# Written order through the last attention chunk, a later routing step and three plane buffers, in an attention + mixture-of-experts kernel

## The chip, the cores and the metric

One core of a Trainium2 chip runs the whole kernel. The metric is device time in microseconds (us) of one execution; lower is better.

## The reference

Eight batches of 1856 rows go through an attention without softmax, the result gates `u`, and all 14848 rows go through a two-level top-1 mixture of 16 experts.

```python
scores = (1 / S) * z @ z.T                      # S = 1856, z: [S, 64]
x = u * (np.maximum(scores, 0) ** 2 @ v)        # u, v: [S, 256]
g_idx = argmax(x @ w_group); e_idx = argmax(x @ w_expert[g_idx])
out = g_w * e_w * (relu(x @ w1[g, e]) @ w2[g, e])   # w1: [256, 1024], w2: [1024, 256]
```

`g_w` and `e_w` are the softmax weights of the chosen group and expert.

## The kernel before

**Attention.** Each batch is cut into four chunks of queries (512, 512, 512 and 320 wide in batches 1 to 7), and each chunk runs over 15 tiles of 128 keys. One key step is one number `s`; there are NS = 480 steps, and the last batch has steps 420 to 479, 15 for each chunk. `attn_v(s)` is TensorE's part (L408): six products, or four where the key tile is the short last one, of 512 or 320 columns. Its operands are the high part `ah` and the low part `al` of the squared scores. They are made six steps ahead by `scores`: for some key tiles from new scores (L370 to L385), for the others from a mirrored tile that an earlier chunk wrote to DRAM and that four DMAs bring back as `at` (`load_mirror`, L326; then `ah` on ScalarE at L359 and `al` on VectorE at L360). In the last chunk (steps 465 to 479, NK = 15) twelve of the fifteen steps use mirrored tiles, and steps 476 to 479 use those of the third mirrored group.

**End of a chunk.** `chunk_end` multiplies by `u` into `xT` (L430, one buffer) and puts off the rest by some steps: `split_x` makes `xh` on ScalarE (L436), `rest_x` makes `xl` on VectorE (L441), `planes` copies `xT` into a plane buffer `pl` on ScalarE (L465) and has SP transpose it into `rows` (L471), `logits` runs four products on TensorE (L483, L484), and `logits_out` copies them out and has SP transpose them into `lgx` (L494). A plane buffer (tag `pl`) also takes the rows of a block of tokens when `load_x` reads them back from the DRAM array `bucket` (L767).

**Routing.** `route` is a generator; `run_gens` lets it advance by a few operations in each step. About 13 small VectorE operations, a pause of 9, 5 or 1 steps, two small products `pk` on TensorE (L610, L611), some more VectorE operations that end in the row numbers `di`, and then one indirect DMA on GpSimd for each 128 rows (L646). The last batch has three such generators, one after the other: chunks 0 and 1 together, chunk 2, chunk 3. After them comes the final sort of the experts.

**Experts.** The first two blocks of tokens (512 rows of each of the two fullest experts) are fixed before the last batch is routed, so they are computed while that routing goes on: `load_rows(0)` and `join_x(0)` (L781 to L787) stand in the last attention steps, `phase1` (L802 to L813) and `phase2_t` (L887) of blocks 0 and 1 follow the attention, with a call of `early` after each eighth of a phase 1 and before each half of a phase 2; a call of `early` is one more step for the generators, four operations at most. What is left of the generators is written out after phase 1 of block 1. The rows of block 2 can be read only when every row of the last batch is in `bucket`.

**What sets the order.** From step 15 on, TensorE, ScalarE and VectorE take their instructions in the order in which the program writes them (`manual_schedule`), up to step 465. Everything after that, and SP and GpSimd throughout, is put in order by a planner: on each engine it takes the instruction that stands first in the program among those that it holds to be ready by its own reckoning of time. From the block pairs (`duo`) on, all engines are in written order again.

Of the kernel before, what the change touches and what calls it, by code (L numbers as in the profile page):

```python
# [9 lines left out]
F32 = mybir.dt.float32  # L10
# [3 lines left out]
U16 = mybir.dt.uint16  # L14
# [5 lines left out]
P = 128  # L20
# [4 lines left out]
def f32(ap):  # L25
    return ap.bitcast(F32)
# [3 lines left out]
def tile_glu_attn_moe(  # L30
# [12 lines left out]
    B, D, S = uT.shape  # L43
    DQ = zT.shape[1] // 2
    NE, _, F = w1.shape
# [5 lines left out]
    NK = NKF + 1  # L51
# [39 lines left out]
    def sb(tag, shape, dt, bufs, name):  # L91
        return pool.tile(shape, dt, tag=tag, bufs=bufs, name=name)
# [19 lines left out]
    def new_rows(name):  # L112
        return sb("rows", [P, 4, RW], I32, 4, name)

    def new_pl(name):
        return sb("pl", [P, 2048], U16, 2, name)

    def new_xhl(name):
        return tuple(new_vb(f"{h}_{name}").rearrange("p (d q) -> p d q", d=ND) for h in ("xh", "xl"))
# [222 lines left out]
    NS = len(steps)  # L342
# [77 lines left out]
    def chunk_end(s):  # L420
        b, c, k = steps[s]
        w = QW[b][c]
        last = s == NS - 1
        nt = (w + P - 1) // P
        oa = oacc.pop(s - k)
        u_t = ut.pop((b, c))
        xT = sb("xT", [P, ND, 512], F32, 1, f"xT_{b}_{c}")[:, :, 0:w]
        xhl = []
        for d in range(ND):
            nc.vector.tensor_mul(out=xT[:, d, :], in0=oa[d][:, 0:w], in1=u_t[:, d, :])  # L430

        def split_x():
            xhl.extend(new_xhl(f"{b}_{c}"))
            xh, xl = xhl
            for d in range(ND):
                nc.scalar.copy(out=xh[:, d, 0:w], in_=xT[:, d, :])  # L436

        def rest_x():
            xh, xl = xhl
            for d in range(ND):  # L440
                nc.vector.tensor_sub(out=xl[:, d, 0:w], in0=xT[:, d, :], in1=f32(xh[:, d, 0:w]))  # L441

        rows = new_rows(f"rows_{b}_{c}")
        nc.gpsimd.iota(rows[:, 0:nt, D + 1:RW], pattern=[[P, nt], [0, RW - D - 1]],
                       base=b * S + QO[b][c], channel_multiplier=1)
        part = w % P
        pl = new_pl(f"pl_{b}_{c}").rearrange("p (t g q) -> p t g q", t=4, q=P)
        lgp = sb("lgp", [P, 512], F32, 1, f"lgp_{b}_{c}").bitcast(U16)[0:LP].rearrange("p (t h q) -> p t h q", t=4, q=P)
        if c % 2 == 0:
            duo[b, c // 2] = (rt_("lgx", [8, 2, LP], f"{b}_{c}", U16), [])  # L450
        lgx2, parts2 = duo[b, c // 2]
        lgx = lgx2[:, 4 * (c % 2):4 * (c % 2) + nt]
        parts2.append((rows, nt, part))
        if nt < 4:
            nc.gpsimd.memset(lgx2[:, 4 * (c % 2) + nt:4 * (c % 2) + 4], 0)
        if part:
            nc.gpsimd.memset(pl[:, nt - 1, :, part:P], 0)
            nc.gpsimd.memset(lgp[:, nt - 1, :, part:P], 0)

        def planes(d):  # L460

            for t0, t1, q in ((0, w // P, P), (w // P, nt, part)):
                if t1 > t0:
                    src = xT[:, d, t0 * P:t0 * P + (t1 - t0) * q].bitcast(U16)
                    nc.scalar.copy(  # L465
                        out=pl[:, t0:t1, 2 * d:2 * d + 2, 0:q],
                        in_=src.rearrange("p (t q h) -> p t h q", q=q, h=2),
                    )
            if d == ND - 1:
                for t in range(nt):  # L470
                    nc.sync.dma_start_transpose(  # L471
                        rows[:, t, 0:D].bitcast(U16).rearrange("p (g d) -> p g d", d=P),
                        pl[:, t].rearrange("p g q -> p (g q)"),
                    )

        pls = []

        def logits():
            ps = bank(ps_m, "m", f"pl_{b}_{c}")
            pls.append(ps)  # L480
            xh, xl = xhl
            for d in range(ND):
                nc.tensor.matmul(ps[0:LP, 0:w], whl[:, d, :], xh[:, d, 0:w], start=(d == 0), stop=False)  # L483
                nc.tensor.matmul(ps[0:LP, 0:w], wh0[:, d, :], xl[:, d, 0:w], start=False, stop=(d == ND - 1))  # L484

        def logits_out():
            ps = pls[0]
            for t0, t1, q in ((0, w // P, P), (w // P, nt, part)):
                if t1 > t0:
                    src = ps[0:LP, t0 * P:t0 * P + (t1 - t0) * q].bitcast(U16)  # L490
                    nc.scalar.copy(
                        out=lgp[:, t0:t1, :, 0:q], in_=src.rearrange("p (t q h) -> p t h q", q=q, h=2)
                    )
            nc.sync.dma_start_transpose(  # L494
                lgx.rearrange("p t h l -> p (t h) l"), lgp[:, 0:nt].rearrange("p t h q -> p (t h q)")
            )

        LG = (7 if b == B - 1 and c < 2 else (9 if c == 2 else 8 if c == 0 else 7)) if s + 1 < NS - NK else 2
        XO = 2 if s + 1 < NS - NK else 0
        (split_x() if XO == 0 else defer(s + XO, split_x))  # L500
        (rest_x() if XO == 0 else defer(s + XO + 1, rest_x))
        PL = XO + 1 if not XO or c == 2 else LG + 2
        defer(s + PL, lambda: planes(0))
        defer(s + PL + 1, lambda: planes(1))
        defer(s + LG, logits)
        defer(s + LG + (1 if XO else 0), logits_out)
        wait = 5 if last else 12 if b == 0 and c < 2 else (17 if c == 1 and b < B - 1 else 15) if s + 1 < NS - NK else 8
        alone = b == B - 1 and c >= NQ - 2
        if c % 2 or alone:
            gens.append((max(s + wait, PFILL[-1] + 2), route(b, c // 2, (c % 2,) if alone else (0, 1))))  # L510
        if last_sort(b, c):
            gens.append((0, sort_experts()))
        if last:
            gens.append((0, sort_experts(final=True)))
# [305 lines left out]
    def phase2(name, wt, hs, meta, n, outs, between=None):  # L820
        nt = (n + P - 1) // P
        held = same if name == "ov" else pin
        for at, t in enumerate([nt - 1] + list(range(nt - 1)) if half(n) else range(nt)):
# [7 lines left out]
            one = name == f"w{NE - 1}_1" and t == nt - 1  # L831
# [7 lines left out]
            for f in range(0 if pair else NF):  # L839
                w2t = wt["2"][f // 2][:, (f % 2) * 512:(f % 2 + 1) * 512]  # L840
                held(nc.tensor.matmul(py[0:m, 0:D], hs[f][1][:, ts], w2t[:, 0:D], start=False, stop=(f == NF - 1)))
            y = sb("yl", [P, D], F32, 3, f"y_{name}_{t}")
            cw = meta[0:m, t, 0:1].bitcast(F32)
            top = py[0:m, 0:D]
            if pair:
# [139 lines left out]
    for b in range(1, B):  # L985
        for what, n, load, cut in PREP if b > 1 else PREP0:
            s0 = (b - 1) * NQ * NK
            begin.setdefault(s0 + load[0] * NK + load[1], []).append((what, b, n))
            split_at.setdefault(s0 + cut[0] * NK + cut[1], []).append((what, b, n))
    WPREP = ((2, (2, 3), (2, 9)), (0, (2, 4), (2, 12)), (1, (2, 5), (2, 14)), (3, (3, 0), (3, 6)))  # L990
    xs = []
    ahead = 4
    for s in range(ahead):
# [7 lines left out]
    for s in range(NS):  # L1001
        b, c, k = steps[s]
        if s == NK:
            region.enter_context(tc.manual_schedule(engines={mybir.EngineType.PE, mybir.EngineType.Activation, mybir.EngineType.DVE}))
        if s == NS - NK:
            region.close()
        if s in (1, 4):
            pz.pop(0)()
        if s in (2, 6, 9):
            pv.pop(0)()  # L1010
        if s == 8:
            make_router()
        for i in range(2 * NE):
            if PFILL[i] == s:
                prefill(i)
        nxt = s // NK + 1
        if k == 3 and nxt < B * NQ:
            load_ut(nxt // NQ, nxt % NQ)
        if b + 1 == B:
            for pc, load, cut in WPREP:  # L1020
                if (c, k) == load:
                    wts.setdefault(0, new_w())
                    prep[pc] = load_w(regs(0)[0], wts[0], pc, "e0")
                if (c, k) == cut:
                    prep.pop(pc)()
        for what, pb, n in begin.get(s, ()):
            prep[(what, n)] = (prep_v if what == "v" else prep_z)(pb, n)
        for what, pb, n in split_at.get(s, ()):
            prep.pop((what, n))()
        if k == (5 if s < NK else 5) and nxt < B * NQ:  # L1030
            prep_zm(nxt // NQ, nxt % NQ)
        if s == NS - NK - 6:
            load_rows(0)
        if s == NS - 6:
            load_rows(1)
        if s == NS - 12:
            xs.append(join_x(0, rows_b[0][0], blocks[0][2]))
        while ahead < min(NS, s + LEAD + 1, max(4, 3 + s + s // 2)):
            scores(ahead)
            ahead += 1  # L1040
        attn_v(s)
        if k == NK - 1:
            chunk_end(s)
        run_deferred(s)
        run_gens(s, 2 if b + 1 < B else (3 if c < 3 else 5))
# [339 lines left out]
    for i, (e, r0, n) in enumerate(blocks):  # L1385
# [20 lines left out]
        last = i + 1 == NB  # L1406
# [67 lines left out]
    for e in range(NOLD, NE):  # L1474
# [36 lines left out]
        B = ("0 0 x0 T2 T4; 0 5 x3 x2l; 0 9 x5 x1; 0 14 x4; 0 18 x6; 1 3 sv; 1 8 sa; 1 11 go; 1 12 m; 1 14 m; 1 18 m; 1 21 m")  # L1511
# [92 lines left out]
```

## Time and profile before

| what | value |
|---|---|
| median of 3 runs | 1426.38 us (1425.99 to 1427.35) |
| the profiled execution, its own time | 1423.95 us |
| its span, first to last instruction | 1422.1 us |
| TensorE (PE) busy | 1411.9 us, 99% of the span |
| VectorE (DVE) busy | 1216.5 us, 86% |
| ScalarE (ACT) busy | 1051.3 us, 74% |
| GpSimd (POOL) busy | 439.0 us, 31% |
| TensorE's granted clock, mean | 1.000 of full speed |

Matmuls are pipelined: each is shown for some 0.3 to 0.4 us, but the next starts after 0.15 to 0.23 us. So a short wait can hide inside a "busy" PE, and the starts of two matmuls say more than the busy time.

### The profile page before, as it was taken

Reading aid. Unit: us, or ns where it says so; the run is one execution under the profiler, and the core shown is the slowest. Engines: PE = TensorE matmul, PEld = TensorE weight load, DVE = VectorE, ACT = ScalarE, POOL = GpSimd, SP = SyncE. Lnnn points to the kernel's source line nnn. Section 1 sums busy time; section 2 is a strip of 40 time slices with the busy share of each in tenths; the row PEclk is TensorE's granted clock in tenths of the full one; section 3 lists DMA queues with packets and bytes.
Section 4 is the critical chain, followed back from the end, with each engine's and each line's share of the span. In section 5 each row is a group of like instructions: output and inputs, shape, how many; then the busy total and the mean of one; then the engine's idle time right before and its main releaser. Section 6 shows DMA issues by size and latency. Waiting matters only on the chain.

```text
span 1422.1 us, 22589 instructions
## 1 busy us (share of the span) xinstructions
PE 1411.9 (99%) x7010; PEld 1223.8 (86%) x7010; DVE 1216.5 (86%) x2436; ACT 1051.3 (74%) x1849; POOL 439.0 (31%) x462
## 2 busy tenths in 40 slices
PE   9999999999999999999999999999999999999998
PEld 7898888888888888888878898988888888899997
DVE  7889999899998999998988667789777888888884
ACT  8887887787887878878776354357777777777773
POOL 0002022220222012202222331332445555555554
PEclk9999999999999999999999999999999999999999
DMA  9997979979899698895987564534555444555552
GB/s 318 328 260 210 235 187 254 230 192 239 195 262 238 160 264 207 223 244 151 243 197 165 116 142 113 122 82 130 126 136 132 126 123 113 138 137 136 139 140 60
DMA packets 400043, 256.47 MB, mean 180 GB/s; under 512 B 244131, under 2 KB 355262, under 8 KB 399920
## 3 DMA queue, kind: packets, MB, share of 16 engines
q1 hardware_dynamic: 387984, 223.97, 63.1%
q0 software_dynamic: 11856, 30.90, 7.7%
q8 instruction: 56, 0.92, 0.3%
q14 instruction: 67, 0.55, 0.1%
q10 hardware_dynamic: 80, 0.13, 0.0%
HBM read 108.29 MB, written 89.21 MB: 139 GB/s over the span
## 4 chain that ended last, share of the span: by engine, by line
PE 92%; DVE 2%; DMA 2%; issue 2%; POOL 1%; ACT 1%; SPq 0%; POOLq 0%; DVEq 0%; ACTq 0%
PE o L408 38%; PE duo_p L887 15%; PE yT L887 6%; PE duo_y L1333 6%; PE sc L370 5%; PE sc L371 5%; PE ph L802 2%; PE ph L803 2%; PE ph L804 2%; PE duo_w L1333 2%; PE duo_x L1333 2%; PE duo_p L1333 2%; PE duo_z L1333 2%; PE pl L483 1%; PE pl L484 1%
## 5 line engine op out<-in xcount | busy, mean ns | idle before, releaser
L408 PE MATMUL o<-ah,vl 128*128 128x512 f32 (+2 forms) x960 | 354.6, 370 | 0.4 <-DVE ah L382 0.4
L408 PE MATMUL o<-ah,vh 128*128 128x512 f32 (+2 forms) x960 | 354.2, 369 | 0.0
L408 PE MATMUL o<-al,vh 128*128 128x512 f32 (+2 forms) x896 | 328.7, 369 | 0.9 <-DVE al L360 0.9
L646 POOL DMA_INDIRECT bucket<-rows,di x121 | 138.6, 1145 | 383.3 <-issue 216.7
L374 ACT ACTIVATE r<-sc 128x512 f32<-128x512 f32 (+2 forms) x312 | 178.8, 573 | 74.4 <-PE sc L371 72.8
L408 PEld LDWEIGHTS o<-ah,vl 128*128 128x128 f32 x960 | 180.2, 188 | 31.0 <-DVE ah L382 1.2
L408 PEld LDWEIGHTS o<-ah,vh 128*128 128x128 f32 x960 | 180.2, 188 | 28.9
L385 DVE TENSOR_TENSOR al<-r,ah 128x512 fp32r<-128x512 f32 (+2 forms) x280 | 187.7, 671 | 19.1 <-ACT r L379 2.2
L930 POOL DMA_INDIRECT out_dram<-y_w,meta_w x92 | 139.3, 1514 | 191.4 <-ACT y_w L924 145.8
L408 PEld LDWEIGHTS o<-al,vh 128*128 128x128 f32 x896 | 167.8, 188 | 27.5 <-DVE al L360 1.2
L887 PE MATMUL duo_p<-hh_w,duo_w 128*128 128x496 f32 (+10 forms) x692 | 178.0, 371 | 0.0
L381 ACT ACTIVATE r<-r 128x512 f32<-128x512 f32 (+2 forms) x280 | 171.4, 612 | 8.9
L887 PEld LDWEIGHTS duo_p<-hh_w,duo_w 128*128 128x128 f32 x692 | 128.6, 188 | 16.7
L382 DVE CAST ah<-r 128x512 fp32r<-128x512 f32 (+2 forms) x280 | 115.9, 414 | 18.8 <-ACT r L381 13.4
L370 PE MATMUL sc<-zm,z2h 128*128 128x512 f32 (+2 forms) x312 | 120.0, 385 | 0.2 <-DVE zm L251 0.2
L371 PE MATMUL sc<-zm,z2l 128*128 128x512 f32 (+2 forms) x312 | 118.9, 381 | 0.0
L310 DVE STREAM_TRANSPOSE mt<-r 128x512 f32<-128x512 f32 x147 | 103.6, 705 | 0.6
L887 PE MATMUL duo_p<-hl_w,duo_w 128*128 128x496 f32 (+10 forms) x346 | 104.1, 371 | 0.0
L360 DVE TENSOR_TENSOR al<-at,ah 128x512 fp32r<-128x512 f32 (+1 forms) x168 | 95.3, 579 | 2.5 <-ACT ah L359 2.3
L359 ACT CAST ah<-at 128x512 fp32r<-128x512 f32 (+1 forms) x168 | 86.1, 531 | 8.8 <-DMA at<-sym 3.9
L807 ACT ACTIVATE hh<-ph 128x512 fp32r<-128x512 f32 (+6 forms) x96 | 45.7, 488 | 39.4 <-PE ph L804 38.6
L887 PE MATMUL yT<-hh,w_e 128*128 128x512 f32 (+6 forms) x352 | 74.1, 328 | 0.0
(259 smaller groups left out, 2874.5 us busy)
## 6 DMA issues: line engine op xcount, KB each, us to landing
sym<-mt SPq DMA_DIRECT2D x126, 256.0 KB
duo_r<-in_w_dram SPq DMA_DIRECT2D x48, 512.0 KB
at<-sym SPq DMA_DIRECT2D x84, 256.0 KB
bucket<-padrow SPq DMA_DIRECT2D x32, 660.0 KB
at<-sym SPq DMA_DIRECT2D x84, 160.0 KB
vr<-in_v_dram SPq DMA_DIRECT2D x23, 512.0 KB
ut<-in_uT_dram SPq DMA_DIRECT2D x23, 512.0 KB
raw_e<-in_w_dram SPq DMA_DIRECT2D x16, 512.0 KB
```

Source lines behind the costliest of these rows:

```text
L310: nc.vector.transpose(out=t2.rearrange("p (j t x) -> p t j x", t=KT, x=32), in_=a.rearrange("p (t j x) -> p t j x", t=KT, x=32))
L370: held(nc.tensor.matmul(ps[:, 0:w], z2h[:, ks], zm, start=True, stop=False))
L371: held(nc.tensor.matmul(ps[:, 0:w], z2l[:, ks], zm, start=False, stop=True))
L374: held(nc.scalar.activation(out=a, in_=ps[:, 0:w], func=AF.Relu, scale=1.0 / S))
L381: held(nc.scalar.activation(out=a, in_=a, func=AF.Square))
L382: held(nc.vector.tensor_copy(out=ah, in_=a))
L385: held(nc.vector.tensor_sub(out=al, in0=a, in1=f32(ah)))
L408: held(nc.tensor.matmul(oa[d][:, 0:QW[b][c]], (vh if q else vl)[:, d0:d0 + P], al if q == 2 else ah, start=(i == 0 and q == 0), stop=end a ...
L646: nc.gpsimd.indirect_dma_start(out=views[(b * NQ + 2 * half + hs[h]) * NT + i], out_offset=bass.IndirectOffsetOnAxis(ap=di[0:n, i0 + i:i0 ...
L887: nc.tensor.matmul(o, wt["2"][f // 2][:, w0:w0 + P], hs[f][q // 2][:, c0:c0 + n], start=(at == 0), stop=(at == 3 * NF - 1))
L930: nc.gpsimd.indirect_dma_start(out=outs(), out_offset=bass.IndirectOffsetOnAxis(ap=meta[0:m, t, 1:2], axis=0), in_=y[0:m], in_offset=None, ...
L1333: nc.tensor.matmul(out, a, b, start=(q == 0 and m in (1, 5)), stop=(q == 2), skip_group_check=True)
```

## The change

It moves the end of the first written stretch from step 465 to step 479, so that the written order also holds for the last chunk except its last step; it starts the routing of chunks 0 and 1 of the last batch at step 472 in place of 464; it gives the plane buffers a third copy; and it shifts some steps around it: the logits of chunk 1 by two, the split, planes and logits of chunk 2 to where the other chunks have them, the loads and splits of expert 0's weights, and `load_rows(0)` and `join_x(0)` by three.

```diff
     def new_pl(name):
-        return sb("pl", [P, 2048], U16, 2, name)
+        return sb("pl", [P, 2048], U16, 3, name)
...
-        LG = (7 if b == B - 1 and c < 2 else (9 if c == 2 else 8 if c == 0 else 7)) if s + 1 < NS - NK else 2
-        XO = 2 if s + 1 < NS - NK else 0
+        LG = (7 + 2 * c if b == B - 1 and c < 2 else (9 if c == 2 else 8 if c == 0 else 7)) if not last else 2
+        XO = (1 if (b, c) == (B - 1, 0) else 2) if not last else 0
...
-        PL = XO + 1 if not XO or c == 2 else LG + 2
+        PL = XO + 1 if not XO or c == 2 else LG + (0 if (b, c) == (B - 1, 1) else 2)
...
-        wait = 5 if last else 12 if b == 0 and c < 2 else (17 if c == 1 and b < B - 1 else 15) if s + 1 < NS - NK else 8
+        wait = 5 if last else 12 if b == 0 and c < 2 else (17 if c == 1 and b < B - 1 else 23 if b == B - 1 else 15) if s + 1 < NS - NK else 8
...
-            y = sb("yl", [P, D], F32, 3, f"y_{name}_{t}")
+            y = sb(*(("yl", [P, D], F32, 1) if one else ("y", [P, D], F32, 3)), f"y_{name}_{t}")
...
-    WPREP = ((2, (2, 3), (2, 9)), (0, (2, 4), (2, 12)), (1, (2, 5), (2, 14)), (3, (3, 0), (3, 6)))
+    WPREP = ((0, (2, 3), (2, 12)), (1, (2, 4), (2, 14)), (2, (2, 5), (3, 2)), (3, (3, 6), (3, 11)))
...
-        if s == NS - NK:
+        if s == NS - 1:
             region.close()
...
-        if s == NS - NK - 6:
+        if s == NS - NK - 3:
             load_rows(0)
         if s == NS - 6:
             load_rows(1)
-        if s == NS - 12:
+        if s == NS - 9:
             xs.append(join_x(0, rows_b[0][0], blocks[0][2]))
```

## Rows read from the trace of the kernel before

**Rows 1.** PE, DVE, ACT, POOL: busy us and instructions in stretches of 50 us.

```profile
650.00:700.00 50.00, 50.00 (x253) 42.98 (x252) 46.50 (x105) 41.91 (x79) 9.76 (x13) 1.00 0.72 184
700.00:750.00 50.00, 48.74 (x235) 40.39 (x234) 41.93 (x98) 36.63 (x63) 7.72 (x9) 1.00 0.83 196
750.00:800.00 50.00, 49.06 (x233) 39.74 (x232) 40.82 (x123) 25.86 (x48) 17.57 (x17) 1.00 0.65 151
```

**Rows 2.** Timeline of PE near 730: start, length in us, instruction, [idle before, releaser].

```profile
728.49 0.40 PE L483 MATMUL pl<-xh,whl 128*48 128x512 f32 x1
730.14 0.44 PE L484 MATMUL pl<-xl,wh 128*48 128x512 f32 x1 [1.26 <-DVE xl L441]
...
731.01 0.39 PE L408 MATMUL o<-ah,vl 128*128 128x512 f32 x1
```

**Rows 3.** Timeline of VectorE near 730.

```profile
729.35 1.34 DVE L441 TENSOR_TENSOR xl<-xT,xh 128x512 fp32r<-128x512 f32 x2
```

**Rows 4.** Timeline of PE in the last attention chunk.

```profile
742.82 0.31 PE L408 MATMUL o<-ah,vl 128*128 128x320 f32 x1
...
743.70 0.31 PE L408 MATMUL o<-ah,vl 128*128 128x320 f32 x1
...
751.13 0.40 PE L484 MATMUL pl<-xl,wh 128*48 128x512 f32 x1
...
753.28 0.56 PE L408 MATMUL o<-al,vh 128*128 128x320 f32 x2 [0.94 <-DVE al L360]
753.67 0.31 PE L408 MATMUL o<-ah,vl 128*128 128x320 f32 x1
```

**Rows 5.** Timeline of ScalarE in the last attention chunk.

```profile
748.55 1.05 ACT L465 COPY pl<-xT 128x1024 uint16<-128x1024 uint16 x1 [2.97 <-DMA rows<-pl]
...
752.87 0.46 ACT L359 CAST ah<-at 128x320 fp32r<-128x320 f32 x1 [0.17 <-DMA at<-sym]
753.23 1.05 ACT L786 CAST xh_m<-xf 128x1024 fp32r<-128x1024 f32 x1
```

**Rows 6.** Timeline of VectorE in the last attention chunk.

```profile
743.20 0.48 DVE L360 TENSOR_TENSOR al<-at,ah 128x320 fp32r<-128x320 f32 x1
...
750.16 0.69 DVE L441 TENSOR_TENSOR xl<-xT,xh 128x512 fp32r<-128x512 f32 x1 [3.00 <-ACT xh L436]
...
751.29 1.33 DVE L781 COPY xf<-xp 128x2048 uint16<-128x2048 uint16 x1
...
754.41 1.22 DVE L787 TENSOR_TENSOR xl_m<-xf,xh_m 128x1024 fp32r<-128x1024 f32 x1
```

**Rows 7.** Timeline of SP's queue in the last attention steps.

```profile
735.75 5.06 SPq L767 DMA_TRANSPOSE xp<-bucket  x1
...
747.45 2.03 SPq L326 DMA_DIRECT2D at<-sym  x4
```

**Rows 8.** Instructions of L767: durations in ns, least, median, longest.

```profile
L767 SPq DMA_TRANSPOSE xp<-bucket x12: 1231/1378/5062, 735.7 to 908.2; - x12
```

**Rows 9.** Timeline of PE in blocks 1 and 2.

```profile
781.16 0.39 PE L802 MATMUL ph<-xh_m,w1l_e 128*128 128x512 f32 x1
...
788.05 0.20 PE L610 MATMUL pk<-oh,tri 128*128 128x64 bf16 x1
...
788.87 0.20 PE L611 MATMUL pk<-pre,ones 128*128 128x64 bf16 x1
...
803.36 0.33 PE L802 MATMUL ph<-xh_m,w1l_e 128*128 128x384 f32 x1
```

**Rows 10.** Timeline of GpSimd: indirect DMAs of the last chunk's rows.

```profile
791.12 0.95 POOL L646 DMA_INDIRECT bucket<-rows,di  x1 [2.68 <-issue]
...
793.65 0.90 POOL L646 DMA_INDIRECT bucket<-rows,di  x1 [0.30 <-issue]
```

**Rows 11.** Timeline of SP: rows of block 2 are read.

```profile
795.96 1.45 SPq L767 DMA_TRANSPOSE xp<-bucket  x1
```

**Rows 12.** Timeline of ScalarE: high part of block 2's rows.

```profile
800.71 0.83 ACT L786 CAST xh_m<-xf 128x768 fp32r<-128x768 f32 x1 [7.43 <-DVE xf L781]
```

## The prediction

> **What bounds the kernel now.** I read the page first, then the busy time in stretches of 50 us, then the timelines of PE, ScalarE, VectorE, SP and GpSimd between 716 and 840 us. TensorE sets the time nearly everywhere. In the written stretch before the last batch it is busy without a gap; the two stretches that hold the edited steps lack 1.26 and 0.94 us [rows 1]. Since pipelined matmuls hide part of a wait, I count starts. A 512-column product takes 0.229 us from start to start (30 of them from 781.16 to 788.05 [rows 9]), a 320-column one 0.147 us (six from 742.82 to 743.70 [rows 4]). So there are two places to win:
>
> - At 728.49 the first logits product of chunk 1 runs and the second waits for `xl` [rows 2, 3]. To 731.01 there are four products, 0.92 us of work in 2.52 us: 1.60 us lost.
> - From 751.13 to 753.67 one 512- and six 320-column products, 1.11 us of work, take 2.54 us: 1.43 us lost, ended by `al` on VectorE [rows 4].
>
> Behind the second is a chain: ScalarE idles 2.97 us before `planes` of chunk 2, until the transposes of chunk 1's planes are done [rows 5]; `xh` stands behind that, VectorE idles 3.00 us for it, and `xf` and routing operations then go ahead of the late `al` [rows 6]. Nothing else of size is lost beside start and tail, so no version can win much more than 3 us, 0.2% of the time.
>
> **The change part by part.**
>
> *Logits of chunk 1, steps 456 to 458.* Two steps later is two times six products of 0.229 us, 2.7 us. `xl` ends at 730.69 [rows 3]; the logits would then start at about 731.2, after it. VectorE's order up to there is not edited. Gain 1.60 us.
>
> *Third plane buffer, and chunk 2 like the others.* Chunk 1's planes, block 0's rows and chunk 2's planes now have one buffer each, so the 2.97 us on ScalarE go, and with them the 3.00 us of VectorE. `xh` also comes ahead of `planes`. Gain: the 1.43 us, if nothing else makes `al` late. Together 3.03 us.
>
> *Written order in the last chunk.* Before, the planner could put a ready product in front of a waiting one, and in the last attention steps it did so with phase 1 of block 0. Now step 478 must run before anything of the experts. What is late is then paid by TensorE at once. The operand most at risk is the third mirrored group, for steps 476 to 479: SP issued it at 747.45, behind the transposes, and `ah` still waited for it at 752.87 [rows 5, 7]. Behind `ah` of step 476 the new order has, in a row: its `al` 0.48, `xf` 1.33 on VectorE, `xh_m` 1.05 on ScalarE, `xl_m` 1.22 and `al` of step 477 0.48 on VectorE [rows 5, 6]. If the group lands no sooner than before, `al` of step 477 is there at 752.87 + 0.46 + 0.48 + 1.33 + 1.05 + 1.22 + 0.48 = 757.9. TensorE, 1.6 us earlier than before, starts chunk 3 at 741.2, and after twelve steps of 0.88 and the logits of 0.92 it wants step 477 at 752.7 and its `al` two products later, at 753.0. Then 4.9 us are lost: the upper bound. The lower is nothing: in the last chunk of the batch before, written too, TensorE has no gap [rows 1]. Between them stands the one transposition of `xp` that took 5.06 us where the median of its line is 1.38 [rows 7, 8]; it is ahead of the mirrored group on SP, and three weight loads are queued there too. Now the transposes of chunk 1 can go first and the queue has time to drain. Without the 3.7 us of excess the group lands 3.7 us sooner and 1.2 us are lost. I take 1.2.
>
> A rule of the Trainium skill speaks against this part: in PSUM — Partial Sum Buffer, section Engine vs sequencer instructions, the queues of ScalarE and VectorE are strictly first in, first out, and matmuls start in program order. The trace agrees: `xh` sat behind the waiting `planes` for the 2.97 us [rows 5]. By that rule alone, with the group as late as before, the sum would be the upper bound's.
>
> *Routing eight key steps later.* It takes 14 small VectorE operations from steps 464 to 467 and puts them into steps 472 to 474, partly in front of `al` of step 479, where the next chunk no longer covers them; I count them in the bounds above. Its second effect lies later. The generators run one after the other, a call of `early` is worth four operations, and I count them through. Before, the `pk` products of chunk 2 are written after phase 1 of block 0, and those of chunk 3 after the fifth eighth of phase 1 of block 1. After, all come seven calls later: chunk 2's stand where chunk 3's stood, and chunk 3's after the whole phase 1 of block 1. The trace shows that the planner keeps the written place when operands are ready: chunk 3's first `pk` runs at 788.05, exactly 30 products after the block's start, the fifth eighth [rows 9].
>
> From that place P the old chain was: second `pk` P + 0.82, first indirect DMA 2.25 later, three DMAs 1.265 apart, the last ends at 794.55, SP reads the rows at 795.96, and `xh_m` of block 2 is ready at 801.54, 6.99 us after the last indirect DMA [rows 9 to 12]. That is P + 13.5. TensorE wanted it at 803.36, P + 15.3: 1.8 us to spare. The new chain has chunk 2's `pk` at P, both at once since their inputs are long done, so the first indirect DMA at P + 2.3. Then come four DMAs of chunk 2 and three of chunk 3: the last starts 6 x 1.265 = 7.6 later and ends at P + 10.8, and `xh_m` is ready at P + 17.8. TensorE, which has the same work after P, wants it at P + 15.3. So 2.5 us are lost before block 2. Bounds: nothing, if the planner finds room for `pk` or GpSimd earlier; 4.0, if the second `pk` comes 0.8 later as before and chunk 3's `di` comes after chunk 2's DMAs. I take 2.5, since the place in the program is what the trace follows.
>
> *The rest.* The weight loads keep their three early transfers together; their order changes nothing while ScalarE has other work, and one split put too early would hold ScalarE by some fraction of a transfer (inside the bounds above). `load_rows(0)` and `join_x(0)` later: block 0 starts after step 478 now, and its `xh_m` is in the chain above. The `y` tags share three buffers with earlier results, whose DMAs were issued several products before; GpSimd's DMAs cover that at 1.265 us each [rows 10], which is also what it would cost once if that cover were gone.
>
> *Sum*, against the profiled execution's own 1423.95 us (span 1422.1 and 1.85 us around it): -1.60 - 1.43 + 1.2 + 2.5 = +0.7 us, 1424.6. The median of the runs lies 2.43 us over that execution, so 1427.0 us.
>
> **The rivals.**
>
> *Both waits stay away.* The group lands early enough, and the indirect DMAs are done in time since the attention ends some microseconds earlier and chunk 2's routing can use VectorE sooner. For it: the gapless written chunks before [rows 1]. Against it: `pk` stands at a place in TensorE's order, so an earlier end of the attention moves both sides. It gives -3.0: 1423.4 us, faster by 0.21%.
>
> *The mirrored group is as late as before.* Place: `ah` of step 476; price 4.9 us in place of 1.2. Sum -3.03 + 4.9 + 2.5 = +4.4: 1430.8 us, slower. It decides (over 0.2%, 2.85 us) once the group lands after some 751.3, 3.4 us of loss. For it: the landing at 752.87 [rows 5]; against it: the free plane buffers and the one long transposition that may not come again [rows 8].
>
> A rule of the Trainium skill bears on this one, in DMA: Bandwidth & Descriptors, section Queues, rings and completion order: what SP issues goes through one row of rings, consumed in ring order. [...] By it the group cannot overtake the weights, and the time would be this rival's.
>
> *The change does not do what it says*: SP stays with the planner, which may still put `xp` and the transposes so that `planes` waits. Then the 1.43 us stay and the result is about +2, inside the forecast's band.
>
> **How the numbers follow.** A measurement of this kernel tells about 0.2%, 2.85 us, from no change. Forecast, the gain given back at block 2 and step 477, with the last rival: 0.50; both waits away: 0.22; the late group: 0.28. Only the second ends faster by over 0.2% and only the third slower, so 0.22, 0.50, 0.28. The range goes from the whole gain with a little of the small gaps, -3.6, to the late group with its bound hardly reached, +4.8: 1422.8 to 1431.2. The forecast's own range is 1424.0 to 1429.2.
>
> **What would show it.** Right: no wait before the second logits product of chunk 1; no 2.97 us before `planes` of chunk 2; a gap of 1 to 2 us on PE in steps 476 to 478, released by VectorE or the mirrored tiles; `pk` of chunk 2 after the fifth eighth of block 1, seven indirect DMAs in a row behind it, and a gap of some 2.5 us on PE before the first product of block 2. Wrong: the indirect DMAs of chunk 2 before phase 1 of block 1 ends its fifth eighth (then no loss there), or a gap of 4 us and more within the last chunk.

## The result and the profile after

The changed kernel takes 1440.39 us (median of 5 runs, 1440.20 to 1441.08) beside 1426.38 of the kernel before: a ratio of 1.0097, 95% interval 1.0086 to 1.0108, 14 us slower. The forecast was 1427.0 with a range up to 1431.2: wrong, and by far. Its profiled execution took 1440.2 us, with a span of 1438.5 and a mean granted clock of 0.996.

Busy time in stretches says where to look. Columns: stretch, its length, busy us and instructions of PE, weight loads, VectorE, ScalarE, GpSimd, then PE's granted clock, DMA share, GB/s.

```profile
725.00:750.00 25.00, 25.00 (x127) 21.47 (x126) 22.82 (x48) 20.59 (x37) 6.24 (x9) 1.00 0.82 192
750.00:775.00 25.00, 21.55 (x103) 17.87 (x102) 16.70 (x46) 12.18 (x26) 0.64 (x2) 0.93 0.82 182
775.00:800.00 25.00, 25.00 (x114) 19.95 (x113) 19.43 (x60) 12.48 (x21) 8.77 (x9) 1.00 0.28 77
800.00:825.00 25.00, 16.63 (x74) 14.05 (x73) 11.19 (x31) 4.93 (x7) 9.78 (x10) 0.86 0.48 110
...
760.00:763.50 3.50, 3.50 (x10) 2.73 (x9) 3.36 (x9) 0.96 (x4) 0.00 (x0) 0.51 0.89 121
...
818.00:821.50 3.50, 3.45 (x11) 3.45 (x12) 3.12 (x7) 0.00 (x0) 1.17 (x2) 0.51 0.39 87
```

725 to 750 has no gap now, where the kernel before lost its 1.6 us. The loss sits in the last chunk and before block 2, each time first as idle PE and then as a stretch at a granted clock of 0.51, the lower level of 1.2 GHz. The timeline of PE names the operands that it waited for, in brackets behind a row. It is to be read against [rows 2, 4, 9]:

```profile
734.52 0.39 PE L484 MATMUL pl<-xl,wh 128*48 128x512 f32 x1
...
754.49 0.31 PE L408 MATMUL o<-al,vh 128*128 128x320 f32 x1
756.78 0.41 PE L408 MATMUL o<-ah,vl 128*128 128x320 f32 x1 [1.98 <-ACT ah L359]
...
759.63 0.50 PE L802 MATMUL ph<-xh_m,w1l_e 128*128 128x512 f32 x1 [1.47 <-ACT xh_m L786]
...
763.61 0.31 PE L408 MATMUL o<-ah,vl 128*128 128x320 f32 x1
...
785.72 0.22 PE L611 MATMUL pk<-pre,ones 128*128 128x128 bf16 x1
...
798.08 3.33 PE L887 MATMUL yT<-hh,w_e 128*128 128x512 f32 x14
...
802.52 0.20 PE L611 MATMUL pk<-pre,ones 128*128 128x64 bf16 x1
...
804.88 0.73 PE L887 MATMUL yT<-hh,w_e 128*128 128x512 f32 x2 [1.84 <-ACT hh L807]
...
811.13 0.39 PE L887 MATMUL yT<-hl,w_e 128*128 128x512 f32 x1
818.05 0.69 PE L802 MATMUL ph<-xh_m,w1l_e 128*128 128x384 f32 x1 [6.53 <-ACT xh_m L786]
```

The logits of chunk 1 run without a wait. `ah` of step 476 and then block 0's `xh_m` are late (step 477 follows only at 763.61), and before block 2 PE stands from 811.5 to 818.05. The second `pk` of chunks 0 and 1 runs at 785.72, that of chunk 3 at 802.52, behind the first 14 products of block 1's phase 2. On SP:

```profile
739.05 4.96 SPq L767 DMA_TRANSPOSE xp<-bucket  x1
744.11 5.37 SPq L471 DMA_TRANSPOSE rows<-pl  x4
749.58 1.21 SPq L494 DMA_TRANSPOSE lgx<-lgp  x1
750.89 2.04 SPq L326 DMA_DIRECT2D at<-sym  x4
...
812.52 1.45 SPq L767 DMA_TRANSPOSE xp<-bucket  x1
```

on ScalarE:

```profile
748.45 1.03 ACT L465 COPY pl<-xT 128x1024 uint16<-128x1024 uint16 x1
...
756.27 0.46 ACT L359 CAST ah<-at 128x320 fp32r<-128x320 f32 x1 [5.12 <-DMA at<-sym]
...
804.23 0.60 ACT L807 ACTIVATE hh<-ph 128x512 fp32r<-128x512 f32 x1 [6.48 <-PE pk L611]
```

on VectorE the first operation that reads chunk 3's `pk`:

```profile
805.86 0.23 DVE L614 TENSOR_TENSOR rk<-pk,base 128x64 f32<-128x64 f32 x1 [0.31 <-remote]
```

and on GpSimd the indirect DMAs, fifteen of them:

```profile
788.69 1.09 POOL L646 DMA_INDIRECT bucket<-rows,di  x1 [19.75 <-DVE sm L628]
...
802.73 0.97 POOL L646 DMA_INDIRECT bucket<-rows,di  x1 [0.30 <-issue]
807.52 0.96 POOL L646 DMA_INDIRECT bucket<-rows,di  x1 [3.82 <-issue]
```

The long transposition still stands ahead of the third mirrored group, which SP issues at 750.89 (before 747.45, [rows 7]; PE itself reaches chunk 3 1.2 us later, at 744.04 beside 742.82 [rows 4]). The 2.97 us before `planes` of chunk 2 are gone. Block 2's rows are read at 812.52, 16.6 us later than in [rows 11].

To compare whole runs I add up, for every matmul, the time to the next start minus the median for its width. For the 70 products of 128 columns, whose median is 0.067 us in some runs and 0.106 in others, I take 0.106 in all. The kernel before loses 6.1 us so, the changed one 22.4. The difference of 16.3 is that of the two profiled executions (1440.2 and 1423.95); the medians of the runs differ by 14.0, because the profiled execution of the kernel before lay 2.4 under its median. The table gives this loss by stretch for all runs, one profile each, with the ratio to the kernel before, taken on the same chip. Up to 725 us the runs spread from 1.3 to 6.0 though the order there hardly differs, and the two profiles of the changed kernel differ by 2.3 between 775 and 825: a profile says nothing below some 2 us.

| kernel | to 725 | 725 to 775 | 775 to 825 | ratio (95%) |
|---|---|---|---|---|
| before | 1.3 | 3.3 | 0.5 | 1 |
| changed | 4.4 | 6.0 | 11.1 | 1.0097 (1.0086 to 1.0108) |
| changed, once more (e13) | 3.0 | 6.0 | 13.4 | 1.0097 (1.0082 to 1.0113) |
| routing at 15 (e1) | 3.0 | 8.6 | 0.6 | 1.0028 (1.0019 to 1.0037) |
| split of chunk 0 back (e2) | 6.0 | 4.1 | 12.5 | 1.0098 (1.0082 to 1.0115) |
| no written order in the last chunk (e3) | 3.5 | 3.7 | 8.3 | 1.0050 (1.0037 to 1.0063) |
| both e1 and e3 (e10) | 1.5 | 4.4 | 0.4 | 1.0011 (1.0002 to 1.0020) |
| last logits at 5 (e8) | 2.0 | 4.1 | 8.2 | 1.0067 (1.0054 to 1.0081) |
| block 0's rows late (e7) | 1.5 | 0.9 | 8.2 | 1.0044 (1.0031 to 1.0058) |
| e7 and e8 (e16) | 4.1 | 1.4 | 10.1 | 1.0038 (1.0026 to 1.0050) |
| routing at 19 (e9) | 1.6 | 7.2 | 1.8 | 1.0030 (1.0020 to 1.0041) |
| e7, routing at 15 (e12) | 4.3 | 4.8 | 0.7 | 1.0002 (0.9993 to 1.0011) |
| e7, routing at 19 (e11) | 2.8 | 5.4 | 1.7 | 1.0019 (1.0009 to 1.0028) |
| e7, routing at 20, 8 a call (e15) | 2.3 | 4.3 | 0.4 | 0.9991 (0.9983 to 1.0000) |
| e15, join earlier (e17) | 2.1 | 3.1 | 0.5 | 0.9996 (0.9987 to 1.0005) |
| before, later logits (e4) | 2.1 | 3.6 | 3.0 | 1.0001 (0.9990 to 1.0011) |
| before, third plane buffer (e5) | 4.9 | 3.7 | 3.0 | 1.0011 (1.0002 to 1.0020) |
| before, later logits and rows (e14) | 3.9 | 8.5 | 0.5 | 1.0024 (1.0015 to 1.0032) |

In the last stretch the runs that lose more than 10 us (changed, e13, e2, e16) are those in which ScalarE is held before a `hh`: it stands idle for some 5 to 6.5 us though the product that it needs has run, as at 804.23 above. Those with the late routing but without this hold (e3, e7, e8) lose 8.2 or 8.3. Its cause is open (last section).

### The profile page after: what moved, and what is told of

The parts are those of the page before. It is cut to its first block, busy times and chain, and to the rows that moved or that the text cites. A ratio compares the mean times of both kernels' runs of the same rounds, so it can differ in the third digit from the quotient of the medians.

```text
span 1438.5 us, 22568 instructions
## 1 busy us (share of the span) xinstructions
PE 1416.8 (98%) x7010; PEld 1226.7 (85%) x7010; DVE 1216.3 (85%) x2436; ACT 1047.5 (73%) x1849; POOL 433.6 (30%) x462
## 4 chain that ended last, share of the span: by engine, by line
PE 92%; DVE 2%; issue 2%; POOL 2%; DMA 1%; ACT 1%; SPq 0%; POOLq 0%; DVEq 0%
PE o L408 39%; PE duo_p L887 14%; PE duo_y L1333 6%; PE yT L887 5%; PE sc L370 5%; PE sc L371 5%; PE ph L802 2%; PE ph L803 2%; PE ph L804 2%; PE duo_w L1333 2%; PE duo_x L1333 2%; PE duo_p L1333 2%; PE duo_z L1333 2%; PE pl L483 1%; PE pl L484 1%
## 5 line engine op out<-in xcount | busy, mean ns | idle before, releaser
L646 POOL DMA_INDIRECT bucket<-rows,di x121 | 133.9, 1106 | 388.2 <-issue 215.9
L887 PEld LDWEIGHTS duo_p<-hh_w,duo_w 128*128 128x128 f32 x692 | 128.6, 188 | 16.6
```

What stands on the lines that cost most here:

```text
L646: nc.gpsimd.indirect_dma_start(out=views[(b * NQ + 2 * half + hs[h]) * NT + i], out_offset=bass.IndirectOffsetOnAxis(ap=di[0:n, i0 + i:i0 ...
L887: nc.tensor.matmul(o, wt["2"][f // 2][:, w0:w0 + P], hs[f][q // 2][:, c0:c0 + n], start=(at == 0), stop=(at == 3 * NF - 1))
```

## The experiments

**Routing back to 15 steps (e1).**

```diff
-        wait = ... (17 if c == 1 and b < B - 1 else 23 if b == B - 1 else 15) ...
+        wait = ... (17 if c == 1 and b < B - 1 else 15) ...
```

> The changed kernel with the routing of the last batch's first half started 15 steps after its chunk again, as before, in place of 23; all else as changed. Theory (three places): the late routing puts `pk` of chunks 0 and 1 behind chunk 3's logits on the one bank `ps_m`, 785.65 in place of 766.46, the twelve indirect DMAs start 18 us late, and block 2 waits 6.7 us, with 1.6 us of half clock behind it and the 2.1 us before chunk 3's `pk`: 10.4 us go, 1430.0. Rival (the written order of the last chunk is the whole cause): `pk` only moves within a stretch where GpSimd has time, the time stays at 1438 or more. Rival (the DMAs only catch up in part): 1433 to 1436, with a wait of some 2 to 4 us left before block 2.

1431.52 us beside 1426.79, 1.0028. 9.8 of the 13.8 us go, as the theory had it: the first indirect DMA starts at 773.01 in place of 788.69, and block 2 does not wait. But the last chunk lost more than with the late routing. On VectorE and on PE:

```profile
750.15 0.52 DVE L548 COPY lgf<-lgx 128x640 uint16<-128x640 uint16 x1 [5.51 <-DMA lgx<-lgp]
...
751.30 0.48 DVE L360 TENSOR_TENSOR al<-at,ah 128x320 fp32r<-128x320 f32 x1
```

```profile
751.84 0.41 PE L408 MATMUL o<-al,vh 128*128 128x320 f32 x1 [3.44 <-DVE al L360]
```

Under the written order VectorE's first routing operation waits 5.51 us for a transpose, `al` of the attention stands behind it, and PE waits 3.44 us. So the parts of the change belong together: with the written order an early routing costs in the last chunk, a late one before block 2.

**Chunk 0 split two steps after its chunk (e2).**

```diff
-        XO = (1 if (b, c) == (B - 1, 0) else 2) if not last else 0
+        XO = 2 if not last else 0
```

> The changed kernel with the split of the last batch's first chunk two steps after its chunk again, as before, in place of one; all else as changed. Theory: `xh` of that chunk then no longer stands on ScalarE in front of the `r` of a key step, and the 1.74 and 0.61 us at 699 and 608 us go: 1438.0, and everything later moves by the same amount. Rival (the step only moves a wait; the scores' bank would be late by itself, since VectorE is the one that is late): 1440. Rival (the late third mirrored group comes from these 2.4 us, as SP issues it 3.4 us later than before): the 5.5 us of the last chunk go too, 1433.

1.0098, no gain: a miss. The waits moved (1.5 us at 706, others before 600). The changed kernel, run a second time, shows what they are worth:

> The changed kernel once more, unedited, beside the others on one chip. Theory: the waits of the last chunk (some 4 to 6 us with its half clock) and before block 2 (6 to 8 us with its half clock) are there again; those at 608, 699 and 802 us, which are not found in other kernels with the same order up to there, are not the change's and come or go: 1.007 to 1.010. Rival (they belong to the split of the first chunk one step earlier): 0.6, 1.7 and 2.1 us at these places again.

The ratio came out the same, the waits of the last chunk and before block 2 are there, the 1.7 us at 699 are not (the one at 608 is 0.27). So that wait is no price of the change. The one at 802 came back, with 3.4 us, so the theory was wrong on that.

**The planner sets the last chunk again (e3).**

```diff
-        if s == NS - 1:
+        if s == NS - NK:
             region.close()
```

> The changed kernel with the written order ending 15 steps before the last, as before, so that the planner sets the whole last chunk; all else as changed. Theory: the waits for `ah` at 756.78 and for `xh_m` at 759.63 and the half clock behind them go (2.15 + 1.63 + 1.7 = 5.5 us), the wait before block 2 stays: 1434.9. Rival (the written order is the whole cause): 1426 or less. Rival (it is no cause, the third group is late for both orders): 1439 to 1441.

1.0050, 1434.33 us beside 1434.9 expected. 3.7 us are lost in the last chunk, about as before the change, and PE still waits 5.02 us before block 2. The hold of `hh` is also absent here, so the 6.7 us that go by the ratios are not the written order's alone: 2.3 of them show in the last chunk.

**Both undone (e10).**

The edits of e1 and e3 together.

> The changed kernel with two parts undone together: the routing 15 steps after its chunk and the written order ending 15 steps before the last, both as before; the later logits, the third plane buffer and the rest stay. Each alone was measured: the routing back 1431.5 us, the order back 1434.3, neither 1440.4. Theory (the routing's delay costs at the bank and the DMAs, the written order costs in the last chunk, and early routing under the written order costs there too, since its first operation waits for a transpose with all of VectorE behind it): 1423.5 to 1425.5, what the later logits win and the planner keeps. If the two losses only added, it would be 1431.5 + 1434.3 - 1440.4 = 1425.4. Rival (the third plane buffer and SP's new order cost something of their own): 1427 or more.

1.0011. As expected the two parts carry nearly the whole loss, but 1.0011 of 1426.4 is 1428, the rival's side: the later logits and the third plane buffer, which stay in, win nothing.

**The last chunk's logits behind `pk` on the bank (e8).**

```diff
-... else 8 if c == 0 else 7)) if not last else 2
+... else 8 if c == 0 else 7)) if not last else 5
```

> The changed kernel with the logits of the last chunk five steps after it in place of two, so that on the one bank `ps_m` they come after `pk` of chunks 0 and 1 and not ahead of them; the routing stays at 23 steps, the written order stays. Theory (the bank's order holds the routing up, more than its eight steps): `pk` runs some 15 us earlier than 785.65, the first eight indirect DMAs end before `di` of chunk 2, and only the loss of the forecast stays before block 2, seven DMAs in a row and some 2.5 us: 1440.4 - 4.2 (6.7 to 2.5 there) - up to 3.7 (the 2.1 at 802 and the half clock, if these hang on the same) = 1432.5 to 1436. Rival (the routing's eight steps alone make `pk` late): 1439 to 1441. Rival (chunk 3's routing, now later, takes the place): 1440 or more, with its `pk` later than 802.5.

1.0067, 4.3 us better. `pk` of chunks 0 and 1 runs at 769.37 in place of 785.72 (2.4 of it since this run lost less up to 725) with the routing at 23 as it was: the bank held it. Yet PE waits 4.71 us before block 2 where 2.5 were expected. Chunk 3's second `pk` on PE, with the end of block 1, and the first of its three indirect DMAs:

```profile
797.14 0.20 PE L611 MATMUL pk<-pre,ones 128*128 128x64 bf16 x1
...
804.52 0.39 PE L887 MATMUL yT<-hl,w_e 128*128 128x512 f32 x1
809.62 0.69 PE L802 MATMUL ph<-xh_m,w1l_e 128*128 128x384 f32 x1 [4.71 <-ACT xh_m L786]
```

```profile
799.03 0.96 POOL L646 DMA_INDIRECT bucket<-rows,di  x1 [3.20 <-issue]
```

From that `pk` to block 2's first product are 12.5 us; in [rows 9, 12] `xh_m` was ready 12.7 us after it. The DMAs of chunk 2 were long done, GpSimd stood idle 3.20 us. So the place of chunk 3's `pk` decides, not the row of seven DMAs.

What the 4.3 us consist of is another matter. By stretch e8 loses 2.9 less between 775 and 825, where the hold of `hh` is absent, and 1.9 less in the last chunk, where the same two waits (1.60 and 1.48 us) were not followed by the lower clock. Neither is shown to come from the bank, and e7, next, keeps the bank's order and loses the same 8.2 us before block 2.

**Block 0's rows seven steps later (e7).**

```diff
-        if s == NS - NK - 3:
+        if s == NS - 11:
             load_rows(0)
```

> The changed kernel with the rows of block 0 loaded seven steps later, so that on SP the transposition of `xp` for block 0, 4.96 us, comes behind the third mirrored group and not ahead of it. Theory (the group's place on SP behind a transposition is the cause in the last chunk): the group lands some 5 us earlier, the wait for `ah` of step 476 (2.15 us) goes; the wait for `xh_m` (1.63 us) may grow since `xp` is later, or go with the products of block 0 behind the attention; half clock 1.7 us less or not: 1435 to 1438. Rival (the group waits for a buffer, not for its place): 1440. Rival (`xp` late costs as much as the group early gives): 1440 to 1443, with a wait for `xh_m` of 4 us and more.

1.0044, 7.5 us better by the ratios, more than either side expected. SP's queue:

```profile
742.15 1.21 SPq L494 DMA_TRANSPOSE lgx<-lgp  x1
743.46 2.03 SPq L326 DMA_DIRECT2D at<-sym  x4
745.63 2.65 SPq L767 DMA_TRANSPOSE xp<-bucket  x1
```

The group is issued 7.4 us earlier (2.9 of it since this run lost less up to 725), the last chunk loses 0.9 us in place of 6.0, and block 0 waits only 0.3 us for `xh_m`. So 5.1 us of the gain are the last chunk's; between 775 and 825 it is 2.9, where the hold of `hh` is absent. With the group in time and the routing at 23 steps the written order costs under 1 us in the last chunk; what it cannot do is go round a late transfer. Before block 2 this run has no hold, and `pk` of chunks 0 and 1 is still behind the bank (777.72):

```profile
794.53 0.20 PE L611 MATMUL pk<-pre,ones 128*128 128x64 bf16 x1
...
807.15 0.69 PE L802 MATMUL ph<-xh_m,w1l_e 128*128 128x384 f32 x1 [5.75 <-ACT xh_m L786]
```

From the second `pk` of chunk 3 to block 2 are 12.6 us, as in e8. In the changed kernel, with the hold, they are 15.5 (802.52 to 818.05).

**Both repairs (e16).**

The edits of e7 and e8 together.

> The changed kernel with both repairs and nothing else: the rows of block 0 seven steps later (alone 1.0044) and the logits of the last chunk five steps after it (alone 1.0067), routing still at 23 steps. Theory (two separate causes that add up: 1.0097 - 0.0053 - 0.0030): 1.001 to 1.002, the rest being the wait before block 2 that chunk 3's late `pk` makes, some 4.9 us with half clock behind it. Rival (they share time, the earlier attention only lengthens the wait before block 2, which is set by the chain of routing and indirect DMAs): 1.004 as with the first alone.

1.0038: the rival, and no different from e7's 1.0044 within the intervals. Moving `pk` of chunks 0 and 1 ahead on the bank (768.79) leaves the wait before block 2 at 5.8 us, though this run also has the hold. No run shows a price of the bank's order by itself.

**Routing between (e9, e12, e11).** First 19 in place of 23:

> The changed kernel with the routing 19 steps after its chunk in place of 23 (before: 15). In the program `pk` of chunks 0 and 1 then comes ahead of the last chunk's logits on the bank, and all later `pk` one place of three earlier. Theory (the bank's order is the step from cheap to dear, not the count of steps): the wait before block 2 goes nearly as with 15 steps, and the last chunk loses no more than with 23, since the first routing operation waits less for its transpose: 1429 to 1431.5. Rival (cost in proportion to the steps): halfway between 1431.5 and 1440.4, 1436. Rival (the wait on VectorE for that transpose falls in the last chunk as with 15): 1432 to 1434, with waits for `al` on PE of over 4 us.

1.0030, 1428.53 us beside 1424.35. The expected 1429 to 1431.5, beside 1426.4, are ratios of 1.0018 to 1.0036: the theory. Before block 2 it is nearly as with 15 steps, 1.8 us; the last chunk loses 7.2, more than expected: the group comes as late as with 23, and the waits (1.79 and 1.82 us) are followed by the lower clock. The next two add the late rows of e7 to 15 and to 19 steps:

> The changed kernel with two steps put elsewhere: the routing 15 steps after its chunk as before, and the rows of block 0 loaded seven steps later, so that SP issues the transposes of chunk 1, its logits and the third mirrored group ahead of `xp`. Written order and the other parts stay as changed. Theory (the losses are the bank with the late routing, and SP's order ahead of the written chunk): `lgx` of chunk 1 lands some 5 us earlier, so that the early routing does not hold VectorE as it did at 15 steps alone, the third group is in time, and block 2 does not wait; of the 8.6 us that starts lose in the kernel before, the 3 at 728 and 751 go: 0.997 to 0.999 of the time before. Rival (early routing under the written order holds VectorE wherever `xp` stands): 1.002 to 1.004. Rival (`xp` behind the group makes block 0 wait in place of it): 1.000 to 1.002, with a wait for `xh_m` near 757.

> As the run with 15 steps and the rows of block 0 later, but with the routing 19 steps after its chunk. Theory: the last chunk without loss as with 23 steps, and before block 2 the 1.3 us that 19 steps alone showed: 0.998 to 1.000 of the time before. Rival (block 0 now starts earlier and pulls block 2 with it, while the indirect DMAs hang on VectorE's routing): a wait of 3 us and more before block 2, 1.002.

1.0002 and 1.0019, misses both. The last chunk still loses 4.8 and 5.5 us, for VectorE does the routing there ahead of `al` (15) or of block 0's `xf` (19).

**Versions meant to beat both (e15, e17).**

```diff
-... else 23 if b == B - 1 ...
+... else 20 if b == B - 1 ...
...
-        if s == NS - NK - 3:
+        if s == NS - 11:
             load_rows(0)
...
-        run_gens(late["at"], 4)
+        run_gens(late["at"], 8)
```

> The changed kernel with the routing at 20 steps, the rows of block 0 seven steps later, and eight routing operations a call after the attention in place of four. In the program all `pk` then come early enough for block 2 (chunk 3's second some 60 products ahead of it, before 54). Theory: no wait before block 2; in the last chunk what the run with 19 steps and late rows showed, VectorE doing the routing ahead of `xf`, 3 to 5 us: 0.999 to 1.001. Rival (routing one step later than there lets `xf` go first, as with 23 steps): the last chunk without loss too, 0.997.

0.9991, interval up to 1.0000. Block 2 does not wait, the last chunk still loses 4.3 us. With `join_x(0)` at NS - 10:

> As the run with the routing at 20 steps, late rows of block 0 and eight routing operations a call, but with block 0's join (`xf`, `xh_m`, `xl_m`) one step earlier, so that on VectorE `xf` comes ahead of most of the routing. Theory (VectorE's order alone makes TensorE wait 2.3 us for `xh_m` there): that wait and the half clock behind it go, some 3.5 us, and block 2 has no wait still: 0.996 to 0.998 of the time before. Rival (`xp` lands no sooner, so the written VectorE waits for it and what stands behind, `al` of the last steps, is late): 0.999 to 1.001. Rival (phase 1 of block 0, now placed one step earlier in TensorE's order, waits in front of attention steps): 1.001 or more.

0.9996: the wait for `xh_m` is 2.6 us in place of 2.3, as block 0's first product also moved up. No version is shown to be faster than the kernel before.

**The gains alone (e4, e5, e14).** All in the kernel before. e4 takes two lines of the change:

```diff
-        LG = (7 if b == B - 1 and c < 2 else ...
+        LG = (7 + 2 * c if b == B - 1 and c < 2 else ...
...
-        PL = XO + 1 if not XO or c == 2 else LG + 2
+        PL = XO + 1 if not XO or c == 2 else LG + (0 if (b, c) == (B - 1, 1) else 2)
```

e5 takes the third plane buffer and the `y` tags that make room for it, and e14 takes e4's lines and puts `load_rows(0)` at NS - 11 and `join_x(0)` at NS - 9.

> The kernel before with one part alone: the logits of chunk 1 of the last batch two steps later, its planes where they were. Theory: the 1.60 us before the second logits product of chunk 1 go, nothing else moves: 1424.8. Rival (the gain is passed on to the next wait, `al` of the last chunk, which is tied to ScalarE and the planes): 1426.4, with that wait 1.6 us longer.

> The kernel before with one part alone: the third plane buffer, with the results that share buffers for it. Theory of the forecast: the 2.97 us that ScalarE waits before the planes of chunk 2 go, and with them the 1.43 us before `al` of the last chunk: 0.999 of the time before. Rival (the free buffer lets SP take `xp` of block 1 before other transfers, and the wait goes elsewhere): 1.000 to 1.002, with waits of the same sum on PE between 745 and 760.

> The kernel before with two small edits: the logits of chunk 1 two steps later, and the rows of block 0 loaded so late that SP issues the transposes of chunk 1 and the third mirrored group ahead of `xp`. No written order in the last chunk, two plane buffers, routing as before. Theory (the waits at 730 and 752 hang on SP's order and on VectorE, and the logits alone only moved theirs): both go, 2.5 to 3 us, 0.998 of the time before. Rival (VectorE's work in the last chunk is the bound, so that each wait removed comes back as another): 1.000 to 1.001. Rival (`xp` late makes block 0 or the routing late): 1.002 and more, with a wait for `xh_m`.

The ratios are 1.0001, 1.0011 and 1.0024: the forecast's 3 us are not there. In e4 the logits wait no more, but a `pk` does (1.94 us), behind VectorE, which was held for no cause that the profile shows:

```profile
791.14 0.69 DVE L813 SCALAR_TENSOR_TENSOR hl<-ph,hh 128x512 fp32r<-128x512 f32 x1 [6.63 <-issue]
```

In e5 ScalarE's 2.97 us are gone, and PE waits 1.9 us for `ah` of the third group and 1.9 for `xh_m` of block 2. In e14, which moves `xp` but keeps two plane buffers, PE waits 3.9 us for the same `ah`: a miss, with SP's order as wanted, the four transposes of chunk 1 taking 6.30 us from 740.82 and the group issued at 748.52.

## Why the prediction was wrong

**Gain 1, -1.60.** Right at its place: 1.61 us lost from 725 to 750 before, 0.05 after. But alone (e4) it gave nothing.

**Gain 2, -1.43.** The buffer did what was said: no wait before `planes` of chunk 2. The 1.43 us came back as a wait for the third group (e5), which the forecast had only in its term for the written order.

**Written order, taken at 1.2 with bounds 0 and 4.9.** The term failed in its reason for being small. The working said that the transposes of chunk 1 could go first and the long transposition of `xp` would not come again. SP still took `xp` first, and for 4.96 us, so the third group came 3.4 us later than before. The group as late as before, or later, is the second rival's mechanism, and e7 shows it by taking it away. The Trainium skill (DMA: Bandwidth & Descriptors, section Queues, rings and completion order) states that on each DMA engine descriptors are consumed in ring order. That rule was not what held the group here: the trace has it not yet issued, in SP's own row behind the transpositions. Nor did "step 478 must run before anything of the experts" hold. Only the instructions inside the written stretch keep their order among themselves; the planner put block 0's first products (759.63) ahead of step 477 (763.61), and PE waited again, for `xh_m`. The lower clock behind the two waits was not in the working at all: the 512-column products from 760.33 to 763.3 start 0.427 us apart in place of 0.229, some 1.7 us with the first ones. With the waits of 2.15 and 1.63 us, by starts, the term measured 5.5 us, over its bound.

**Routing, taken at 2.5 with a bound of 4.0: the step that failed most.** It measured 10.7 us from 800 to 825. What failed is the path: the working ran the chain to block 2 from chunk 2's `pk` through a row of seven indirect DMAs, and the runs show it running from chunk 3's own `pk`.

- Chunk 3's `pk`. I put it after the whole of block 1's phase 1, rightly, but let its DMAs simply follow chunk 2's. On PE the second of its two products came 4.4 us into phase 2, behind 14 of that phase's products (3.6 us and 10 products in e8). Phase 2 of block 1 takes 10.9 us in the kernel before (792.48 to 803.36), and from `pk` to a ready `xh_m` are 12.7 [rows 9, 12]. At 0.8 us into phase 2 that would have cost 2.6 us, about the forecast; at 4.4 it is 6.2, and at 3.6 it is 5.4. The runs without the hold waited 5.75 (e7) and 4.71 us (e8). The row of DMAs did not decide: in the changed kernel GpSimd stood idle 3.82 us ahead of chunk 3's first.
- The hold of `hh`. PE waits 2.1 us for it at 802, and VectorE, which stands behind it, first reads chunk 3's `pk` 3.3 us after the product (802.52 to 805.86), where it took 0.6 before the change. No step of the working could have it, and its cause is open.
- The lower clock behind the wait, 384-column products 0.32 us apart in place of 0.174, 1.6 to 2.8 us. It was not in the working.

I also forgot `pk` of chunks 0 and 1 on the one bank `ps_m`. In the program it moved from ahead of the last chunk's logits to behind them, and the bank carries that order onto PE: 766.46 became 785.72, and twelve DMAs ran until 803.7. e8 shows that the bank held it. But that delay is not shown to have cost time: e7 keeps it and e16 does not, at 1.0044 and 1.0038.

e1 sets the routing's whole price at 9.8 us by the ratios.

**The rule that VectorE's and ScalarE's queues are strictly first in, first out** (the Trainium skill, PSUM — Partial Sum Buffer, section Engine vs sequencer instructions) is borne out once more: 5.51 us of VectorE behind one `lgf`, with `al` ready to go behind it (e1). It explains why the routing at 15 steps cost time under the written order while the transpose was late; with the rows of block 0 late too it was 1.0002 (e12).

**The range** ended at 1431.2, just above the mirrored rival's 1430.8. That rival let the two terms together reach 7.4 us, and in the stretches 750 to 775 and 800 to 825 the changed kernel loses 16.6 (5.95 and 10.67), where the one before lost 1.7.

## What to carry to other kernels

When a step is moved later, follow each consumer's chain from its own last producer, at the place where that producer runs on the engine, and not from the queue that looks busiest. A long delay is not yet a price: a single-buffered bank put one pair of products 19 us later here, and no run shows that anything waited for it. A written order on compute engines is only as good as the order on the queue that feeds them: here moving one 5 us transposition behind four small DMAs was worth 5.1 us in the last chunk, more than the two waits together that the change removed. And when a gap of 1.5 us on the bounding engine is one of several that hang on the same two helpers, removing it can just move it: three small repairs of the kernel before gave 1.0001, 1.0011 and 1.0024.

## What the runs showed that was not expected

**The lower clock came after some short waits and not after others.** In the changed kernel a PE idle of 2.0 and then 1.5 us, with six products between, was followed by 3.5 us at a granted 0.51, and the 6.5 us before block 2 by 3.5 us at 0.51. But in e2 waits of 1.66 and 1.45 us at the same place were followed by none, nor in e8 (1.60 and 1.48):

```profile
760.00:764.50 4.50, 3.63 (x16) 3.03 (x17) 3.51 (x8) 1.97 (x5) 0.26 (x1) 1.00 0.75 170
```

A single wait of 2.32 us was followed by the lower level (e15, 0.50 from 756 to 759.4), one of 2.61 us was not (e17). In the kernel before the waits of 1.26 and 0.94 us were followed by none. So the length of a wait alone does not tell, and part of the last chunk's loss, 1.7 us, comes and goes with it.

**Engines held with their operands ready.** In the changed kernel `hh` on ScalarE came 6.48 us after the one before it though its product had started at 797.85; PE's semaphore signals, recorded at 797.13, come next at 804.21, while PE itself went on starting products. (That gap in the signals proves little by itself: the trace has only 1561 of some 1657.) The same hold came again in the second run of that kernel, in e2 and in e16, and in e4 ScalarE and VectorE were held (4.93 and 6.63 us), but not in e7, where PE has the same order there. Where it falls, the wait before block 2 is the shorter the longer PE waits for `hh`, but the two together are longer than the wait alone elsewhere: 2.1 + 6.7, 2.9 + 5.1 and 3.7 + 4.8 us in three runs (by starts), beside 5.9 in e7 and 4.9 in e8. What causes it is open; no run here was aimed at it.
